# An mLSTM cell and a multiplicative FFN in one kernel: early steps reordered, weight words loaded ahead of the fifth unit's rows, one output pass of seven units on GpSimd

## The chip, the cores and the metric

The kernel runs on one NeuronCore of a Trainium2 chip. The metric is the device time of one execution in microseconds (us). Before the change three runs gave 424.96, 425.77 and 426.05 us, median 425.77 us.

## The reference

The inputs are q, k, v and o_gate of shape (4, 8, 768, 40), that is batch, heads, steps, head size; i_gate and f_gate of shape (4, 8, 768); and four weight matrices in float32. An mLSTM cell runs over the 768 steps and its result feeds a multiplicative feed-forward network:

```python
for t in range(S):
    m_new = np.maximum(f_gate[:, :, t] + m, i_gate[:, :, t])
    f_stab = np.exp(f_gate[:, :, t] + m - m_new)
    i_stab = np.exp(i_gate[:, :, t] - m_new)
    m = m_new
    C = f_stab[:, :, None, None] * C + i_stab[:, :, None, None] * np.einsum('bhd,bhe->bhde', vt, kt)
    n = f_stab[:, :, None] * n + i_stab[:, :, None] * kt
    h_tilde = np.einsum('bhde,bhe->bhd', C, qt)
    denom = np.maximum(np.abs(np.einsum('bhd,bhd->bh', n, qt)[:, :, None]), 1.0)
    y[:, :, t] = sigmoid(o_gate[:, :, t]) * h_tilde / denom
...
x = y.transpose(0, 2, 1, 3).reshape(3072, 320)
out = ((x @ w1) * (x @ w2) @ w3) @ w_out        # d_ff = 1024
```

## The kernel before

**Units and stages.** The 768 steps are cut into six chunks of 128. A unit is one chunk of one batch entry with all eight heads; unit n is chunk n // 4 of batch n % 4, and there are 24. The loop at line 820 runs over 32 stages s. In stage s TensorE makes the score products q·k of unit s and its contribution to the state, the output products of unit s - 1, the transposes of y of unit s - 2 (`x_trans`), the transposes of k and q of a coming unit (`turn`), and blocks of the FFN. The instructions of each engine run in the order in which they are written; on TensorE this is tied down by `in_order` (line 84).

**What one unit passes through.** SyncE issues the loads of k, q, v (`load`, line 136) and of the output gate (`load_o`, line 151). `turn` transposes k and q on TensorE and ScalarE copies the result out of PSUM. `rows_of_u` (VectorE, line 293) and `weights` (ScalarE, eight Exp instructions, line 298) make the decay weights `pw`, which `masks` (GpSimd, line 305) cuts to a triangle. `weighted` (GpSimd, line 327) makes v times its weight. In `quarter_work` (line 338) TensorE makes the scores `ss` and the state part `pc`; VectorE multiplies scores and weights (line 397); one stage later TensorE makes `ph` and `pi` from them. `outputs` (line 419) then works on VectorE: `h` from `pi` and `ph` (lines 423 to 430), the denominator in three small instructions (lines 438, 440, 441), and two full passes over 128 x 320 elements (lines 443 and 445): gate times reciprocal, then times h, which is y. `decayed` (GpSimd, line 333) and an add on VectorE (line 406 or 404, then 414) move the state on. `twice` (GpSimd, line 475) copies the last 64 columns of y, so that the third transpose of `x_trans` reads 128 columns; ScalarE copies the transposed result into xT (line 486).

**The steps of a denominator are a generator.** `outputs` returns a function `den`; each call of it issues the next step. `quarter_work` calls it between the instructions of the state.

**Weights.** The weight matrices are float64 (a float32 array times a float64 scalar), so each value comes as two 32-bit words, and the kernel makes float32 of them. Each 512 KB piece is loaded (`fetch`, SyncE), its two words are scaled (`scale`, lines 191 and 193 or 195: two ScalarE instructions, or one of ScalarE and one of VectorE when `early`), and joined in two VectorE instructions (`to_f32`, lines 199 and 200; a pair is one `convert`). Of w1 and w2 there are ten pieces, called 0 to 9 here: 0 and 1 are w1, 2 and 3 are w2, 4 is the remaining rows of both, all for the first 512 columns; 5 to 9 are the same for the last 512. `up` (line 618) starts an FFN block: eight matmuls for `pa` (w1), eight for `pb` (w2); `up_rest` (line 631) adds the remaining rows (tile `wr`) in 32 small matmuls, ScalarE copies `pa` to `a_sb` (line 638) and VectorE multiplies (line 639). The blocks of stages 2 and 3 need pieces 0 to 4, those of stages 4 and 5 pieces 5 to 9.

**Fillers.** `warm(n, m, small)` (line 97) issues matmuls whose result nobody reads: n of 128 x (m x 128), and `small` of 64 x 64. Each is carried out as two passes, two rows of the profile.

**Order before.** Piece 0 is scaled and converted in the prologue (lines 590, 592), piece 1 after `rows_of_u(1)` (lines 610, 611), both early. Stage 2 has a long insert, `between` (line 892): fillers, `x_trans(0)` and `x_trans(1)`, pieces 2 to 4, `turn(2)`, the first FFN block, and piece 5. SyncE's loads in stages 1 and 2 are listed at lines 825 to 838; the pieces 5, 6, 7 come ahead of k and q of unit 4, and 8 and 9 behind them. Pieces 6 and 7 are scaled and converted at the end of stage 2, 8 and 9 in stage 3 (`late`, lines 376 and 410).

Of the kernel before, what the change touches and what calls it, by code (L numbers as in the profile page):

```python
# [11 lines left out]
OP = mybir.AluOpType  # L12
# [4 lines left out]
def kernel(  # L17
# [92 lines left out]
    NB, NBQ, NBV = 4, 3, 5  # L110
    N_DVE = N_U = 10
    N_DIAG = 2
    q_all = const.tile([P, NBQ * H * DP], FP, name="q_all")
    qbuf = [q_all[:, i * H * DP:(i + 1) * H * DP].rearrange("p (h d) -> p h d", d=DP) for i in range(NBQ)]
    kbuf = [const.tile([P, H, DP], FP, name=f"kbuf{i}") for i in range(NB)]
# [222 lines left out]
    def quarter_work(s, rest, between, late):  # L338


        rest()

        def part(j, c0, n):
            return cell[j][:, :, c0:c0 + NP * n].rearrange("p x (n d) -> p x n d", d=n)

        ss, pc, pi = part(0, 0, L), part(0, NP * L, D1), part(1, 0, D1)
        ph = [cell[1][:, x, NP * D1:2 * NP * D1].rearrange("p (h d) -> p h d", d=D1) for x in range(2)]
        n = s - 1
        if 0 <= n < NU:
            pw, vt, qT = u_t.pop(n), vbuf[n % NBV], qT_t.pop(n)  # L350
            before = before_t.pop(n)
            if n < N_DIAG:
                warm(1)

            if n < N_DIAG:
                ph = mps([P, H, D1], "ph")
                for hq in range(H):
                    for r in halves:
                        mm(ph[r, hq, :], pw[r, hq, :], vt[r, hq, :])
            for hd in range(H // 2 if n >= N_DIAG else 0):  # L360
                for x, e in quarters:
                    hq = hd if x == e else hd + H // 2
                    mm(ph[x][halves[e], hd, :], pw[halves[x], hq, :], vt[halves[x], hq, :])
            for p in range(NP):
                for hip, x in quarters if n >= B else quarters[1:3]:
                    mm(pi[halves[x], hip, p, :], qT[heads[hip], p, halves[x]], before[x][heads[hip], p, :])
        den = None
        if 0 <= s - 1 < NU:
            den = outputs(s - 1, pi, ph)
            den()  # L370
            if between:
                for _ in range(3):
                    den()
                den = None
                between()
            if late:
                late()
        n, first_read = s, None
        if n < NU:
            c, b = divmod(n, B)  # L380
            kt, vw = kbuf[n % NB], vw_t.pop(n)
            ends = range(2 if c < NT2 - 1 else 1)
            first, second, after = state[b]
            before_t[n] = first, second
            state[b] = after, second, first
            kT, qT, pw = kT_t.pop(n), qT_t[n], u_t[n]
            for p in range(NP):
                for hip, x in quarters:
                    mm(ss[halves[x], hip, p, :], kT[heads[hip], p, halves[x]], qT[heads[hip], p, halves[x]])
            M = D if n else L  # L390
            for p in range(NP):
                for x, e in quarters:
                    if x in ends:
                        mm(pc[e * L:e * L + M, x, p, :], kt[halves[x], 2 * p + e, 0:M], vw[halves[x], 2 * p + e, :])
        if n < NU:
            pv = pw.rearrange("p (n two) t -> p two n t", two=2)
            first_read = nc.vector.tensor_tensor(out=pv, in0=ss, in1=pv, op=OP.mult)
        with tc.issue_after(first_read.ins) if first_read else nullcontext():
            if den:
                den()  # L400
            if n < NU:

                if c:
                    nc.vector.tensor_tensor(out=second, in0=pc[:, 0], in1=second, op=OP.add)  # L404
                else:
                    nc.vector.tensor_copy(out=second, in_=pc[:, 0])
                if len(ends) > 1:
                    decayed(after, second, n, 1)
            if late:
                late()  # L410
            if den:
                den()
            if n < NU and len(ends) > 1:
                nc.vector.tensor_tensor(out=after, in0=pc[:, 1], in1=after, op=OP.add)
            if den:
                done = den()
        return done if den else first_read

    def outputs(n, pi, ph):
        c, b = divmod(n, B)  # L420
        hs = slice(b * H, (b + 1) * H)
        h = sb.tile([P, H, D1], FP, name="h", tag="h")
        nc.vector.tensor_tensor(out=h.rearrange("p (n two) d -> p two n d", two=2), in0=pi,
                                in1=gT[:, c, hs].rearrange("p (n two) -> p two n", two=2).unsqueeze(3)
                                .to_broadcast([P, 2, NP, D1]), op=OP.mult)
        if n < N_DIAG:
            nc.vector.tensor_tensor(out=h, in0=ph, in1=h, op=OP.add)
        for x, e in quarters if n >= N_DIAG else ():
            part = h[halves[x], 0:H // 2] if x == e else h[halves[x], H // 2:H]
            nc.vector.tensor_tensor(out=part, in0=ph[x][halves[e]], in1=part, op=OP.add)  # L430

        den = sb.tile([P, H, 1], FP, name="den", tag="den")

        def steps():
            V = nc.vector
            yield V.tensor_scalar(out=den.bitcast(U32), in0=h[:, :, D:D1].bitcast(U32), scalar1=0x7FFFFFFF, scalar2=None,
                            op0=OP.bitwise_and)
            yield V.tensor_scalar(out=den, in0=den, scalar1=1.0, scalar2=2.0, op0=OP.max, op1=OP.mult)  # L440
            yield V.reciprocal(out=den, in_=den)
            e = o_t.pop(n)
            nc.vector.scalar_tensor_tensor(out=e, in0=e, scalar=1.0, in1=den.to_broadcast([P, H, D]), op0=OP.add, op1=OP.mult)
            y_t[n] = sb.tile([P, DM + REM], FP, name="y", tag="y")
            yield nc.vector.tensor_tensor(out=y_t[n][:, 0:DM].rearrange("p (h d) -> p h d", d=D), in0=h[:, :, 0:D],
                                           in1=e, op=OP.mult)

        done = steps()
        return lambda: next(done)

# [155 lines left out]
    cols_of_u()  # L606
    nc.scalar.copy(out=decay.rearrange("p j c -> p (j c)"), in_=pd)
    rows_of_u(1)
    nc.scalar.activation(out=g, in_=U, func=AF.Exp)
    scale_next(True)  # L610
    convert()

    ffn = ctx.enter_context(tc.tile_pool(name="ffn", bufs=2))


    ab_t = {}

    def up(gr, fs, cs):


        if gr not in ab_t:
# [3 lines left out]
        for p, wt in ((pa, w1), (pb, w2)):  # L625
            for i, f in enumerate(fs):
                for cc in range(KF):
                    mm(p[:, i, :], wt[:, cc, f * 128:(f + 1) * 128], x[:, cc, cs], start=(i == cc == 0), stop=False)
        return pa, pb, x, gr, fs, cs

    def up_rest(pa, pb, x, gr, fs, cs):
# [188 lines left out]
    for s in range(len(n_up)):  # L820
# [3 lines left out]
            load_u(s + 3)  # L824
        if s < 3:
            if s == 2:
                for _ in range(3):
                    fetch(*todo.pop(0))
            load(s + 2, slice(0, 2))
            if s == 1:  # L830
                load_o(2)
            if s == 2:
                for _ in range(2):
                    fetch(*todo.pop(0))
                fetched = 10
            load(s + 2, slice(2, 3))
            if s:
                load_o(s + 2)
        elif s + 2 < NU:
            load(s + 2)  # L840
            load_o(s + 2)
# [36 lines left out]
            seven[0]()  # L878
        now = [ups.pop(0) for _ in range(n_up[s])]
        open_ups = [up(*x) for x in now] if s != 2 else []  # L880
        if s == 3:
            turn(3)
        def rest():
            for x in open_ups:
                up_rest(*x)
# [6 lines left out]
        def between():  # L892
            twice(1)
            weighted(2)
            rows_of_u(3)
            for _ in range(3):
                scale_next()
            for n in range(2):
                x_trans(n)
                if n == 0:  # L900
                    warm(1, small=38)
            for _ in range(3):
                convert()
            turn(2)
            block = up(*now[0])
            weighted(3)
            weights(3)
            masks(3)
            out_gate(2)
            convert()  # L910
            up_rest(*block)

        gated = None
        if s <= NU:
# [3 lines left out]
        with tc.issue_after(gated.ins) if gated else nullcontext():  # L918
# [5 lines left out]
                ab_sums(*summed.pop(0))  # L924
            if NY <= s - 2 < NU:
                x_turn(s - 2)
            for n in () if s == 1 else (s + 2,) if s < B else (s + 2, s + 3) if s == B else (s + 3,):
                if n < N_U:
                    rows_of_u(n)
            if N_DVE <= s + 1 < NU:  # L930
# [3 lines left out]
            if s < len(n_up) - 2 and n_out[s + 1] and s > NU + 2:  # L934
                ab_sums(*summed.pop(0))
        if s == 0:
            weighted(1)
            weights(1)
            masks(1)
            gate_cols(g, gT, nc.scalar.copy)  # L940
# [5 lines left out]
        if s + 1 < N_DVE:  # L946
            while turned < min(s - 1, NY):
                x_trans(turned)
                turned += 1
            if s not in (1, 2):  # L950
                turn(s + 1)
        if s < NU:
            if 0 < s < NU - 1 and s != 2:
# [3 lines left out]
                if 2 < s < N_DVE:  # L957
                    twice(s - 1)
                masks(s + 1)
            if s != 2:  # L960
                out_gate(s)
        if s in (16, 17):
            weight_sums(s - 16)
        if s == B:
# [47 lines left out]
```

## Time and profile before

| what | value |
|---|---|
| runs, us | 424.96, 425.77, 426.05 |
| span of the profiled execution, us | 425.8 (the page gives no other time of it) |
| TensorE matmul busy | 414.1 us, 97% |
| VectorE busy | 313.5 us, 74% |
| ScalarE busy | 150.1 us, 35% |
| GpSimd busy | 154.3 us, 36% |
| HBM read and written | 44.50 and 5.80 MB |

Shares are of the span. PE is TensorE's matmul side, PEld its weight loads, DVE VectorE, ACT ScalarE, POOL GpSimd, SPq SyncE's queue of DMA issues. A matmul row of the profile is one pass. A releaser called "issue" means that the engine waited for nothing that the profile shows. Times in the text without a unit are us from the start of the span.

### The profile page before, as it was taken

What the parts mean: (1) busy time and instruction counts of PE and PEld (TensorE: products, weight loads), DVE (VectorE), ACT (ScalarE), POOL (GpSimd) and SP (SyncE); (2) the same over time, 40 slices, a digit from 0 to 9 for tenths busy, and PEclk for the clock granted to TensorE, in tenths of its full rate; (3) what the DMA queues carried; (4) which work ended last, traced back from release to release, by engine and by line L of the source; (5) the groups of instructions that cost most, each with busy time, mean ns of one, the idle gap of its engine ahead of it and who ended that gap; (6) DMA issues with size and microseconds to landing.
All of it is one profiled execution on the core that took longest, in us unless ns stands there. A gap on an engine that the chain in (4) does not pass through costs nothing.

```text
span 425.8 us, 13079 instructions
## 1 busy us (share of the span) xinstructions
PE 414.1 (97%) x5353; PEld 335.3 (79%) x5353; DVE 313.5 (74%) x635; ACT 150.1 (35%) x404; POOL 154.3 (36%) x211
## 2 busy tenths in 40 slices
PE   7989989999999999999999999999999999999996
PEld 4768878888688788787777778788778879888896
DVE  6676986888949779778736966596868699575971
ACT  4766865567723623630433313032311110210000
POOL 4421342233303303303307751546453587542100
PEclk9989999999999999999999999999999999999999
DMA  8999998598977776985425675756421120000001
GB/s 186 204 173 245 214 144 140 134 193 180 215 183 154 166 182 135 181 164 105 89 80 130 153 141 121 142 133 117 87 44 36 35 39 2 31 2 31 2 32 62
DMA packets 135211, 51.15 MB, mean 120 GB/s; under 512 B 109360, under 2 KB 126960, under 8 KB 135152
## 3 DMA queue, kind: packets, MB, share of 16 engines
q1 hardware_dynamic: 131552, 46.29, 53.9%
q10 hardware_dynamic: 3600, 4.03, 2.7%
q8 instruction: 42, 0.69, 0.7%
q14 instruction: 17, 0.14, 0.1%
HBM read 44.50 MB, written 5.80 MB: 118 GB/s over the span
## 4 chain that ended last, share of the span: by engine, by line
PE 53%; issue 20%; DVE 7%; POOL 7%; SPq 7%; DMA 5%; ACT 1%; POOLq 0%; DVEq 0%
PE cell L92 17%; PE pa L92 12%; PE o L92 8%; PE pb L92 8%; PE p L92 3%; POOL pw L308 3%; SPq L184 3%; DVE w3T L666 2%; PE pt L95 1%; POOL vw L330 1%; SPq L148 1%; DMA raw<-in_moe_w_dram 1%; PE fill L92 1%; POOL raw L659 1%; POOL state L335 1%
## 5 line engine op out<-in xcount | busy, mean ns | idle before, releaser
L335 POOL TENSOR_TENSOR state<-state,decay 128x164 f32<-128x164 f32 x40 | 20.0, 500 | 154.8 <-DVE state L404 129.0
L92 PE MATMUL pa<-xT,w 128*128 128x256 f32 x240 | 60.4, 382 | 0.0
L92 PEld LDWEIGHTS pa<-xT,w 128*128 128x128 f32 x240 | 44.4, 190 | 6.8 <-DVE h L430 0.4
L303 ACT ACTIVATE pw<-pw,aT 128x64 f32<-128x64 f32 x184 | 46.4, 339 | 3.2 <-ACT o_sb L741 1.9
L92 PE MATMUL pb<-xT,w 128*128 128x256 f32 x192 | 45.4, 379 | 0.0
L729 POOL TENSOR_TENSOR ab<-ab,a_sb 128x512 f32<-128x512 f32 x22 | 29.4, 1356 | 32.2 <-DVE ab L684 32.2
L92 PEld LDWEIGHTS pb<-xT,w 128*128 128x128 f32 x192 | 36.4, 190 | 5.0
L711 POOL TENSOR_TENSOR wo<-wo 128x512 f32<-128x512 f32 x22 | 27.4, 1268 | 29.8 <-DVE wo L686 29.8
L92 PE MATMUL pa<-xT,wr 64*64 64x256 f32 x384 | 37.0, 386 | 0.5 <-DVE wr L200 0.5
L92 PE MATMUL wp<-wo,w3T 128*128 128x320 f32 x128 | 35.9, 433 | 1.1 <-DVE ab L639 0.6
L308 POOL TENSOR_SCALAR_AFFINE_SELECT pw<-pw 64x512 f32<-64x512 f32 x48 | 35.8, 746 | 3.0 <-ACT pw L303 1.2
L92 PE MATMUL pb<-xT,wr 64*64 64x256 f32 x384 | 36.4, 380 | 0.0
L92 PE MATMUL cell<-w3o,ab 128*128 128x320 f32 x128 | 35.4, 432 | 0.0
L638 ACT ACTIVATE a_sb<-pa 128x512 f32<-128x512 f32 x24 | 14.3, 598 | 59.0 <-PE pb L92 59.0
L639 DVE TENSOR_TENSOR ab<-pb,a_sb 128x512 f32<-128x512 f32 x24 | 16.4, 688 | 23.2 <-ACT a_sb L638 22.8
L92 PEld LDWEIGHTS wp<-wo,w3T 128*128 128x128 f32 x128 | 23.8, 190 | 10.5 <-DVE ab L639 0.8
L92 PEld LDWEIGHTS cell<-w3o,ab 128*128 128x128 f32 x128 | 24.3, 190 | 9.5
L92 PEld LDWEIGHTS pa<-xT,wr 64*64 64x64 f32 x384 | 18.9, 132 | 15.4 <-issue 8.8
L686 DVE SCALAR_TENSOR_TENSOR a_sb<-pa,wo 128x512 f32<-128x512 f32 x12 | 8.3, 689 | 29.8 <-PE pa L92 29.8
L430 DVE TENSOR_TENSOR h<-cell,h 64x164 f32<-64x164 f32 x88 | 28.6, 326 | 1.6
L92 PE MATMUL po<-w3o,ab 128*128 128x320 f32 x96 | 26.4, 433 | 0.0
L92 PEld LDWEIGHTS po<-w3o,ab 128*128 128x128 f32 x96 | 18.1, 190 | 7.3
(180 smaller groups left out, 846.4 us busy)
## 6 DMA issues: line engine op xcount, KB each, us to landing
raw<-in_moe_w_dram SPq DMA_DIRECT2D x64, 128.0 KB, 3.4
kbuf<-in_k_dram SPq DMA_DIRECT2D x24, 160.0 KB, 4.5
v_all<-in_v_dram SPq DMA_DIRECT2D x24, 160.0 KB, 4.9
o_in<-in_o_gate_dram SPq DMA_DIRECT2D x24, 160.0 KB, 4.8
pw<-U_d SPq DMA_DIRECT2D x28, 128.0 KB, 3.5
raw<-in_moe_w_dram SPq DMA_DIRECT2D x5, 512.0 KB, 6.7
raw<-in_moe_w_out_dram SPq DMA_DIRECT2D x8, 320.0 KB, 4.1
gates<-in_k_dram SPq DMA_DIRECT2D x28, 80.0 KB, 2.5
```

Of the source, the lines that this page charges most:

```text
L92: in_order(nc.tensor.matmul(out, lhsT=lhsT, rhs=rhs, start=start, stop=stop))
L184: nc.sync.dma_start(out=dst, in_=src)
L303: nc.scalar.activation(out=pw[:, h, :], in_=src[:, h, :], func=AF.Exp, bias=aT[:, c, b * H + h:b * H + h + 1])
L308: nc.gpsimd.affine_select(out=pw[r], in_=pw[r], compare_op=OP.is_ge, fill=0.0, base=0, pattern=[[0, H], [1, L]], channel_multiplier=-1)
L335: nc.gpsimd.tensor_tensor(out=new, in0=old, op=OP.mult, in1=decay[:, b * NP:(b + 1) * NP, 2 * c + x:2 * c + x + 1] .to_broadcast([P, NP, D1]))
L430: nc.vector.tensor_tensor(out=part, in0=ph[x][halves[e]], in1=part, op=OP.add)
L638: nc.scalar.mul(out=a_sb, in_=pa, mul=UP ** -2)
L639: nc.vector.tensor_tensor(out=ab_t[gr][j][:, fs[0]:fs[-1] + 1, t0:t0 + a_sb.shape[-1]], in0=pb, in1=a_sb, op=OP.mult)
L666: nc.vector.tensor_tensor(out=dst, in0=p, in1=q, op=OP.subtract)
L686: nc.vector.scalar_tensor_tensor(out=out, in0=p, scalar=UP ** -2, in1=q, op0=OP.mult, op1=OP.add)
L711: aside_by.tensor_tensor(out=kept[j][:, 1:4:2], in0=kept[j][:, 1:3], in1=kept[j][:, 3:4].to_broadcast([128, 2, TH]), op=OP.add)
L729: aside_by.tensor_tensor(out=t[:, f:FO:FH, :], in0=t[:, f:FO:FH, :], in1=a, op=OP.mult)
```

## The change

The change has these parts.

1. In the prologue the scaling and conversion of piece 1 go; `rows_of_u(2)` and `weighted(1)` come instead (from stage 0). At the end of stage 0 ScalarE scales pieces 1 and 2, one ahead of `out_gate(0)` and one behind it, with both halves on ScalarE.
2. In stages 0 and 1 y of the unit is finished ahead of the state's second add (line 414). The filler ahead of the output products of unit 1 has 256 columns, not 512.
3. `between` is reordered: 8 small fillers ahead of `x_trans(0)`; then 2 of 512 columns and 10 small ones where there were 1 and 38; pieces 1 to 4 are converted in a row, then `rows_of_u(3)`; `turn(2)` stands between `pa` and `pb` of the first block; `up_rest` stands ahead of piece 5.
4. SyncE loads pieces 5 to 9 ahead of k and q of unit 4; the gate of unit 3 comes behind these instead of in stage 1. `turn(4)` moves from the end of stage 3 to the middle of stage 4, behind `up`.
5. For units 2 to 8 GpSimd multiplies h by the reciprocal, in place, ahead of `decayed`, and VectorE makes y in one pass. Line 441 comes ahead of line 404 there.

```diff
+    N_POOL = 9
...
             if n < N_DIAG:
-                warm(1)
+                warm(1, 4 >> n)
...
             if den:
                 den()
+                if on_pool(s - 1):
+                    den()
             if n < NU:
...
-            if den:
+            if den and not on_pool(s - 1):
                 den()
+            if den and n < 2:
+                done = den()
             if n < NU and len(ends) > 1:
                 nc.vector.tensor_tensor(out=after, in0=pc[:, 1], in1=after, op=OP.add)
-            if den:
+            if den and n >= 2:
                 done = den()
         return done if den else first_read
+
+    def on_pool(n):
+        return N_DIAG <= n < N_POOL
...
-            yield V.reciprocal(out=den, in_=den)
+            done = V.reciprocal(out=den, in_=den)
             e = o_t.pop(n)
-            nc.vector.scalar_tensor_tensor(out=e, in0=e, scalar=1.0, in1=den.to_broadcast([P, H, D]), op0=OP.add, op1=OP.mult)
             y_t[n] = sb.tile([P, DM + REM], FP, name="y", tag="y")
-            yield nc.vector.tensor_tensor(out=y_t[n][:, 0:DM].rearrange("p (h d) -> p h d", d=D), in0=h[:, :, 0:D],
-                                           in1=e, op=OP.mult)
+            y, hn, all_d = y_t[n][:, 0:DM].rearrange("p (h d) -> p h d", d=D), h[:, :, 0:D], den.to_broadcast([P, H, D])
+            if not on_pool(n):
+                yield done
+                V.scalar_tensor_tensor(out=e, in0=e, scalar=1.0, in1=all_d, op0=OP.add, op1=OP.mult)
+                yield V.tensor_tensor(out=y, in0=hn, in1=e, op=OP.mult)
+            else:
+                nc.gpsimd.tensor_tensor(out=hn, in0=hn, in1=all_d, op=OP.mult)
+                yield done
+                yield V.scalar_tensor_tensor(out=y, in0=e, scalar=1.0, in1=hn, op0=OP.add, op1=OP.mult)
...
     rows_of_u(1)
+    rows_of_u(2)
     nc.scalar.activation(out=g, in_=U, func=AF.Exp)
-    scale_next(True)
-    convert()
+    weighted(1)
...
-    def up(gr, fs, cs):
+    def up(gr, fs, cs, halfway=None):
...
+            if halfway and p is pa:
+                halfway()
...
             if s == 2:
-                for _ in range(3):
-                    fetch(*todo.pop(0))
-            load(s + 2, slice(0, 2))
-            if s == 1:
-                load_o(2)
-            if s == 2:
-                for _ in range(2):
+                for _ in range(5):
                     fetch(*todo.pop(0))
                 fetched = 10
+            load(s + 2, slice(0, 2))
+            if s:
+                load_o(s + 1)
             load(s + 2, slice(2, 3))
-            if s:
-                load_o(s + 2)
+            if s == 2:
+                load_o(4)
...
-        if s == 3:
-            turn(3)
+        if s in (3, 4):
+            turn(s)
...
             twice(1)
             weighted(2)
+            warm(0, small=8)
+            x_trans(0)
+            scale_next()
+            warm(2, small=10)
+            x_trans(1)
+            scale_next()
+            for _ in range(4):
+                convert()
             rows_of_u(3)
-            for _ in range(3):
-                scale_next()
-            for n in range(2):
-                x_trans(n)
-                if n == 0:
-                    warm(1, small=38)
-            for _ in range(3):
-                convert()
-            turn(2)
-            block = up(*now[0])
+            block = up(*now[0], halfway=lambda: turn(2))
             weighted(3)
             weights(3)
             masks(3)
             out_gate(2)
+            up_rest(*block)
             convert()
-            up_rest(*block)
...
-            for n in () if s == 1 else (s + 2,) if s < B else (s + 2, s + 3) if s == B else (s + 3,):
+            for n in () if s < 2 else (s + 2,) if s < B else (s + 2, s + 3) if s == B else (s + 3,):
...
         if s == 0:
-            weighted(1)
             weights(1)
             masks(1)
...
-            if s not in (1, 2):
+            if s not in (1, 2, 3):
                 turn(s + 1)
...
+            if s == 0:
+                scale_next()
             if s != 2:
                 out_gate(s)
+            if s == 0:
+                scale_next()
```

## The prediction

> **What bounds the kernel.** Page first: PE is busy 414.1 of 425.8 us. Then TensorE's waits over the whole run, because 97% busy leaves 11.7 us and the question is where they are.
>
> ```profile
> PE 414.1 (97%) x5353; PEld 335.3 (79%) x5353; DVE 313.5 (74%) x635; ACT 150.1 (35%) x404; POOL 154.3 (36%) x211
> ...
> q8 instruction: 42, 0.69, 0.7%
> ```
> ```profile
> PE cell L92 <- issue: 1.9, 2, 1.5
> PE fill L92 <- POOL ident masks.py:199: 1.6, 1, 1.6
> PE px L95 <- DVE y L445: 1.2, 1, 1.2
> PE wp L92 <- DVE ab L639: 0.6, 1, 0.6
> PE wp L92 <- issue: 0.5, 1, 0.5
> PE pa L92 <- DVE wr L200: 0.5, 1, 0.5
> ```
>
> The same question from 60 us on finds 2.0 us (0.6 + 0.5 + 0.4 + 0.3 + 0.2). So the change can gain only ahead of 60: by a shorter wait, or by less filler, which counts as busy. TensorE's timeline there:
>
> ```profile
> 22.96 0.83 PE L95 MATMUL px<-ident,y 128*128 128x128 f32 x3 [1.19 <-DVE y L445]
> 23.59 4.90 PE L92 MATMUL fill<-ident 128*128 128x512 f32 x78
> 28.41 0.55 PE L95 MATMUL px<-ident,y 128*128 128x128 f32 x3
> ...
> 47.33 0.43 PE L92 MATMUL pa<-xT,wr 64*64 64x256 f32 x1 [0.51 <-DVE wr L200]
> ...
> 59.05 0.35 PE L92 MATMUL cell<-vw,kbuf 64*40 64x41 f32 x12 [1.49 <-issue]
> ```
>
> Look at the second row: 78 filler passes hold TensorE for 4.9 us. The windows of 1 us show why so long: the granted clock fell after the wait.
>
> ```profile
> 22.00:23.00 1.00, 0.04 (x1) 0.04 (x1) 0.97 (x3) 0.98 (x3) 0.57 (x1) 1.00 1.46 157
> ...
> 24.00:25.00 1.00, 1.00 (x2) 0.00 (x0) 0.83 (x4) 1.00 (x3) 0.00 (x0) 0.50 1.13 167
> 25.00:26.00 1.00, 1.00 (x11) 0.57 (x12) 0.97 (x3) 1.00 (x3) 0.24 (x1) 0.50 0.90 150
> ```
>
> Behind the engine columns stands the clock: 0.50 from 23.4 to 26.8. I follow the change to one checkpoint, stage 4's `wr` matmuls (47.33), behind which TensorE is nearly full.
>
> **Prologue.** VectorE loses L193 0.49, L199 0.81 and L200 0.69 and gains a 0.70 transpose ahead of L397 of unit 0, which then waits for `masks(0)` (12.91 + 1.45 = 14.36) instead of starting at 15.29: 0.9 earlier. `ph` of unit 0 can follow from 15.75, the end of its filler, instead of 16.07. But TensorE next stops for "issue" until 18.22, a stop that VectorE does not set, so `ss` of unit 1 ends at 19.26 as before: gain 0. `weighted(1)` needs v of unit 1, landed at 13.8 (8.92 + 4.9), so it does not block GpSimd.
>
> **y of units 0 and 1.** L414's wait (0.54) and its 0.25 leave y(0)'s chain, and GpSimd's masks no longer double L443 and L445 (0.86, 0.82 beside them; 0.49 each in unit 1): y(0) 22.91 to about 21.6. `h` of unit 1 then waits for `pi` (21.78): y(1) 25.62 to 24.8. The halved filler saves nothing, `ph(1)` waits for L397 (19.99).
>
> **What takes that back.** ScalarE now scales piece 2 (landed 10.73 + 7.4 = 18.1) ahead of `weights(2)`: two rows, 1.1 by their pitch (22.40, 22.95, 23.52). So `weights(2)` starts at 20.1 instead of 18.99 and `masks(2)` ends near 23.6 instead of 22.58. `twice(0)` stands behind it on GpSimd, and `px(0)`'s third transpose reads its copy: 23.9 instead of 23.34. The eight fillers (0.5) fit in before that.
>
> **Fillers.** Now 4 wide and 20 small passes. At full clock a wide one takes 0.44 (0.88 for two), at half 0.88; a small one 0.03 at full clock (76 in 2.9 us, 1.4 of it at half). Full: 1.76 + 0.6, so `px(1)` at 26.3. Half until 26.8: 27.7. Before: 28.41. Since `turn(2)` (0.87) no longer lies between `px(1)` and `pa`, the xT copy (0.48) is bare: `pa` at 27.3 or 28.7 against 29.67, and with `turn(2)` inside, `wr` at 31.6 or 33.0 against 33.22. VectorE keeps up: four converts of 1.16 from 24.8, and 0.45 for one beside `weighted(2)` (1.13 for 0.69 at 26.69), end at 29.9.
>
> **What is late next.** Piece 5 is now scaled behind `a_sb`, which is behind `weights(3)`, which needs `rows_of_u(3)`, now after four converts. ScalarE: 30.6 + 2.0 + 0.4 + 0.6 = 33.5 (full clock) or 35.0 against 33.08. With before's own spacing, L397 of unit 2 comes at 35.4 or 36.9 (35.60), piece 7 is done at 40.2 or 41.7 (40.42), and then L639, `h` and piece 8 take 3.84 (41.32 to 45.16): 44.0 or 45.6. `pb` of stage 4 needs piece 8 from its second matmul. Before, `turn(4)` stood ahead of it and filled the time; now TensorE is there at 42.2 and waits. Then 1.5 of `pb`, 0.87 of `turn(4)`, `wr`: 46.4 (46.8 where GpSimd's new pass slows piece 9's convert), or 48.1, against 47.33. **-0.7 or +0.8.**
>
> **The loads.** No DMA is added. Pieces 8 and 9 land ahead of unit 4's rows, about 38 and 40.5 (estimate: piece 7 at 29.72 + 6.9 = 36.6, less 1.1 for the gate taken out, plus 2 to 3 each as before), no longer the last cause. k and q of unit 4 move from 37.8 and 39.4 to about 42.8; `turn(4)` at 45 or later covers that by 2. The gate of unit 3, near 44, is read by `out_gate(3)` (48.48 before); late, it would hold the `kT` copies behind it on ScalarE. Piece 9's buffer is piece 1's, free at 26 now; its load is issued after 30.
>
> **GpSimd's pass.** VectorE saves one of two passes (0.76 + 0.49 becomes 0.5 to 0.76). GpSimd gains a product of 320 columns, 0.74 by `weighted` (328 columns). It is queued ahead of `decayed`, for which L414 waits; y is behind L414. At 73.4: before y ends at 75.85; after, L441 ends 73.7, product 74.5, `decayed` 74.95, L414 75.25, y 75.75 to 76. Nothing gained, and y has cover (done 48.74, read at 50.05). Value 0; bounds -0.6 (the one wait for L639, 0.58) and +0.7 (a full GpSimd product on the path once).
>
> **Instruction blocks.** The "issue" stops have a pattern: 42 instruction packets of 16 KB stand against 10,706 matmul and weight rows, 255 for each. Counting the trace's TensorE rows (semaphore rows too), the four stops lie at rows 448, 1984, 3264 and 4544, each 192 above a multiple of 256. So TensorE stops where a block of 256 runs out ahead of the next one's arrival, in runs of tiny matmuls: with stops taken out, the blocks before the last three ran in 2.45, 2.75 and 2.45 us and cost 1.49, 0.30 and 0.54; two others of 3.47 and 1.92 cost nothing. The change has 38 passes and 38 weight loads fewer in `between`, so every later boundary falls 76 rows later. Counted so, eight blocks run in under 3.5 us (1.88, 1.89 and 2.09 the shortest, at about 79, 123 and 170). At the mean of those five, 0.47, that is 3.7 instead of 2.3: **+1.4**. Bounds: all stops gone, -2.3; or each block waits until 3.3 us after its start (mean of the three that stopped), 7.1 in all, +4.8. I take the mean, since the rows of equal length differ by three times.
>
> The Trainium skill ("Runtime: NRT & Kernel Launch", "Instruction fetch mechanics") has blocks of 256 instructions and calls the crossing mostly hidden; that would make this term 0, but 1.49 at row 1984 shows that it is not hidden here.
>
> The skill ("TensorE: Matmul & The Clock Gate", "What's actually happening") has half clock after an idle window of 3413 ns, windows free-running against the kernel. The trace's 3.4 us agrees; by the free phase both of my clock cases could occur in the same program, and it speaks against thinning the fillers.
>
> **Sum.** Profiled span 425.8, the median of the runs 425.77: no correction. Full clock: -0.7, +1.4, 0: **426.5**.
>
> **Rivals.** *Boundaries fall well*: the stop at 57 goes (-1.5), none comes, and -0.7: 423.6, or 423.0 with the wait for L639 gone. For it: row 1984 falls on sparse matmuls after the shift. Against: eight short blocks. *Half clock*: the wait for `twice(0)` (1.3) ends in a half-speed window, +0.8 for -0.7: 428.0; it decides once the window that holds 20 to 23.4 is again too idle. For it: the same window did so before, and has less filler now. *Block stops, the slower side*: at full clock and 7.1 us of stops, 429.9; slower by over 1.3 from 0.54 us a block on. *The change does not do what it says*: y early, but `px(0)` still waits on GpSimd; this is in my sum, and if `twice(0)` is not late, `px(1)` comes 0.5 earlier, which piece 8 hides.
>
> **Chances.** Forecast 0.38 (its own range 425 to 428), boundaries well 0.30, half clock 0.20, block stops 0.12. 0.3% is 1.3 us, about what a measurement of this kernel can tell from no change. Faster: 0.28 + 0.03 = 0.31; same 0.02 + 0.27 = 0.29; slower 0.08 + 0.20 + 0.12 = 0.40. Range 422.6 to 430.0: from 0.4 under the fast rival's 423.0 to the block rival's end.
>
> **What would show it.** Right: `px(0)`'s third pass waits for L476 near 23.9; `pb` of stage 4 waits for L200 for over 1 us; `wr` of stage 4 at 46 to 48 without a wait; "issue" stops at rows 192 above multiples of 256, none at 57, one near 79 or 123; L414's wait grows from 0.47 to about 0.9 for units 2 to 8. Wrong: no wait at `pb`, or stops elsewhere.

## The result and the profile after

| | before | after |
|---|---|---|
| median, us | 425.46 | 430.33 |
| runs, us | 424.66 to 428.25 (7) | 428.38 to 432.26 (7) |
| span of the profiled execution, us | 425.8 | 429.9 |
| mean granted clock there | 0.996 | 0.991 |

The ratio is 1.0115, 95% interval 1.0080 to 1.0151: the change costs about 4.9 us. The prediction said 426.5 with a range to 430.0; it was wrong. A run's time is 1.9 to 2.4 us above its span (432.18 beside 429.9 here), so the execution of before that was profiled took about 428, as its longest run of seven did, and not 425.77.

The page of after, busy times and instruction packets:

```profile
PE 415.2 (97%) x5315; PEld 336.1 (78%) x5315; DVE 309.4 (72%) x627; ACT 150.2 (35%) x405; POOL 160.7 (37%) x218
...
q8 instruction: 42, 0.69, 0.7%
```

TensorE issues 38 passes fewer and is busy 1.1 us longer, VectorE has lost 4.1 us of work, and neither says why the span grew by 4.1. TensorE's waits do (total, times, longest):

```profile
PE cell L92 <- issue: 5.0, 4, 1.8
PE fill L92 <- POOL ident masks.py:199: 1.6, 1, 1.6
PE px L95 <- issue: 1.3, 1, 1.3
PE wp L92 <- DVE ab L655: 0.6, 1, 0.6
PE pa L92 <- ACT xT L500: 0.6, 1, 0.6
```

The stops put down to "issue" were 2.7 us before (1.9 and 0.5 in its waits, 0.3 at 96.5) and are 6.3 now: 3.6 of the 4.1 us. The single wait on y, 1.2 before, is gone. TensorE's timeline after has the stops and the checkpoint:

```profile
18.61 0.62 PE L92 MATMUL cell<-qT,kT 40*64 40x64 f32 x26 [1.45 <-issue]
24.29 0.90 PE L95 MATMUL px<-ident,y 128*128 128x128 f32 x3
24.98 3.30 PE L92 MATMUL fill<-ident 128*128 128x512 f32 x24
28.21 0.55 PE L95 MATMUL px<-ident,y 128*128 128x128 f32 x3
29.33 1.99 PE L92 MATMUL pa<-xT,w 128*128 128x256 f32 x8 [0.57 <-ACT xT L500]
...
48.92 0.43 PE L92 MATMUL pa<-xT,wr 64*64 64x256 f32 x1 [0.44 <-DVE wr L201]
...
84.97 0.23 PE L92 MATMUL cell<-vw,kbuf 64*40 64x41 f32 x2 [1.78 <-issue]
...
130.66 0.23 PE L92 MATMUL cell<-vw,kbuf 64*40 64x41 f32 x1 [1.28 <-issue]
...
178.42 0.27 PE L95 MATMUL px<-ident,y 128*128 128x128 f32 x1 [1.29 <-issue]
```

The fifth stop is 0.50 at 43.17. By the count of TensorE's rows in the trace the five stand at rows 448, 1216, 2752, 4032 and 5312, each again 192 above a multiple of 256; the stop at row 1984 (59.05 before) is gone. The second thing that differs is the clock. Windows of 1 us (PE, PEld, DVE, ACT, POOL, clock, DMA share, GB/s) show it at half from 19.5, behind the first stop, to 26.4, two windows of 3.4 us where before had one:

```profile
19.00:20.00 1.00, 1.00 (x50) 0.95 (x40) 0.30 (x1) 1.00 (x3) 0.00 (x0) 0.77 1.12 212
20.00:21.00 1.00, 1.00 (x8) 0.35 (x9) 0.89 (x5) 1.00 (x5) 0.15 (x1) 0.50 0.98 93
...
26.00:27.00 1.00, 1.00 (x4) 0.36 (x2) 0.97 (x3) 0.85 (x2) 0.61 (x2) 0.81 1.36 145
```

Behind the longer first stop, the second window and the stop at 43, the checkpoint of the prediction, `wr` of stage 4, is at 48.92 against 47.33.

### The profile page after: what moved, and what is told of

It is laid out like the page before. It is cut to its first block, busy times and chain, and to the rows that moved or that the text cites. A ratio compares the mean times of both kernels' runs of the same rounds, so it can differ in the third digit from the quotient of the medians.

```text
span 429.9 us, 13003 instructions
## 1 busy us (share of the span) xinstructions
PE 415.2 (97%) x5315; PEld 336.1 (78%) x5315; DVE 309.4 (72%) x627; ACT 150.2 (35%) x405; POOL 160.7 (37%) x218
## 4 chain that ended last, share of the span: by engine, by line
PE 88%; DVE 6%; issue 2%; ACT 1%; DMA 1%; SPq 0%; POOL 0%; DVEq 0%; ACTq 0%
PE cell L92 22%; PE pa L92 21%; PE pb L92 14%; PE wp L92 8%; PE o L92 8%; PE po L92 5%; PE p L92 4%; PE px L95 2%; DVE w3T L682 1%; PE pt L95 1%; PE fill L92 1%; DVE pw L786 1%; PE ph L92 1%; ACT pw L304 0%; DMA out_dram<-o_sb 0%
## 5 line engine op out<-in xcount | busy, mean ns | idle before, releaser
L92 PE MATMUL pb<-xT,w 128*128 128x256 f32 x192 | 45.6, 380 | 0.0
L438 DVE TENSOR_TENSOR h<-cell,h 64x164 f32<-64x164 f32 x88 | 28.7, 326 | 1.6
L92 PE MATMUL po<-w3o,ab 128*128 128x320 f32 x96 | 26.4, 434 | 0.0
```

Of the source, the lines that this page charges most:

```text
L92: in_order(nc.tensor.matmul(out, lhsT=lhsT, rhs=rhs, start=start, stop=stop))
```

## The experiments

Four theories. **A**: blocks of 256 TensorE rows; the change moved every boundary behind 28 us by 76 rows, and three now fall in runs of tiny matmuls. **B**: the reordered early part and its half-clock windows. **C**: GpSimd's pass. **D**: the order of the loads, with TensorE held by piece 8. Fillers are used as the probe: their results are read by nobody, and a small one is four rows (two passes, two weight loads). "No window" below are the runs whose mean clock shows no half-clock window (0.999 or 1.000; one window of 3.4 us takes it to 0.996, as in before's profile). Before has a median of 425.49 in 68 such runs of 117 (three of 476 us and more are left out), after 428.72 in 6 of 14.

**Rows back, rows gone.** The first puts the 76 rows back into after, the second takes 76 from before and changes nothing else.

```diff
             x_trans(1)
+            warm(0, small=19)
```
```diff
-                    warm(1, small=38)
+                    warm(1, small=19)
```

> The changed kernel with 19 more small fillers behind the second x transpose: 76 TensorE rows, so that every later instruction boundary lies where it lay before the change. They cost 1.1 us of filler, of which 0.57 lies in the wait for the xT copy. Theory A (instruction blocks): the stops of 1.78, 1.28 and 1.29 us at about 84, 130 and 178 us go, the stop at row 1984 comes back with up to 1.5, so some 2 to 3 us under the changed kernel, 426.5 to 428.5. Theory B (the early reordering itself lost the time, through the half clock and through piece 8): 430 to 431, since the early part is as it was and has more filler. Theory C (GpSimd's pass): no change either, 430 to 431.

Measured: 429.63, ratio 1.0074 [1.0036, 1.0112]; no window, two runs: 426.9. The median contradicted A, the runs at full clock did not; left open here and taken up below.

> The kernel before with 19 small fillers instead of 38 and nothing else: 76 rows fewer, so the boundaries lie as in the changed kernel, with all the old order. Theory A: stops of over 1 us near 80, 125 and 172 us, and 2 to 3 us slower than before, 427.5 to 428.5. Theory B and C: at most 1 us faster, from the shorter filler, or no difference, 424.5 to 425.5.

Measured: 428.71, ratio 1.0074 [1.0034, 1.0114]; no window 427.42. Taking out 19 fillers brings `wr` of stage 4 to 45.92, 1.4 earlier, and costs 3 us. Its timeline and windows show both halves of it, a stop at row 2752 (the row of after's stop at 84.97), and half clock behind it:

```profile
82.38 0.19 PE L92 MATMUL cell<-vw,kbuf 64*40 64x41 f32 x1 [2.13 <-issue]
```
```profile
82.00:83.00 1.00, 0.62 (x6) 0.50 (x6) 0.32 (x1) 0.00 (x0) 0.00 (x0) 1.00 0.55 201
...
84.00:85.00 1.00, 1.00 (x4) 0.74 (x3) 0.75 (x2) 1.00 (x5) 0.91 (x2) 0.50 0.79 168
85.00:86.00 1.00, 1.00 (x4) 0.82 (x3) 0.75 (x2) 1.00 (x6) 0.08 (x1) 0.50 1.23 230
```

**GpSimd's pass** taken out of after, and put alone into before (the hunks of part 5):

```diff
-    N_POOL = 9
+    N_POOL = 2
```

> The changed kernel without GpSimd's pass (no unit takes it); all else stays, TensorE's rows too. Theory A: the time of the changed kernel within 0.5 us, 430, with the same stops. Theory C: back by 1 us or more, 429 or less. Theory B: no difference.

Measured: 432.18, ratio 1.0141 [1.0099, 1.0184], stops of 0.73, 1.22, 1.55 and 1.30. Without the pass after is no faster, so C is not the cause of the loss.

> The kernel before with GpSimd's pass for units 2 to 8 alone. TensorE's rows stay. Theories A and B: the same as before within 0.6 us, since y had cover and the add of the state waits longer by about what the pass saves. Theory C (the pass costs time): 427 or more.

Measured: 427.30, ratio 1.0027 [0.9997, 1.0058]. Its waits and VectorE's timeline show a price at one place:

```profile
PE pa L92 <- DVE wr L201: 1.3, 1, 1.3
```
```profile
45.14 0.97 DVE L200 TENSOR_SCALAR wr<-raw 128x512 uint32<-128x512 uint32 x1
```

The convert of piece 9 runs beside GpSimd's product (45.11, 0.72) and takes 0.97 where the one of piece 8 takes 0.43, so `wr` waits 1.3, not 0.5.

**Loads alone**: the hunks of part 4, put into before.

> The kernel before with part 4 alone: pieces 5 to 9 ahead of k and q of unit 4, the gate of unit 3 behind them, the transposes of unit 4 in the middle of stage 4. TensorE's rows keep their number, so boundaries behind stage 4 stay. Theory A (instruction blocks explain the loss): within 1 us of before, 424.6 to 426.6. Theory D (this part costs time, because piece 8's convert now holds TensorE in stage 4): 426.7 or more. The part's own purpose would show as 0.5 us less, the wait for the second half of wr gone.

Measured: 426.16, ratio 0.9992 [0.9967, 1.0017]: no difference. D falls as a cause by itself.

**Other alignments.** In this order: after with 24 rows fewer in `between`, before with 16 fewer, after with 64 more ahead of `x_trans(0)`:

```diff
-            warm(2, small=10)
+            warm(2, small=4)
```
```diff
-                    warm(1, small=38)
+                    warm(1, small=34)
```
```diff
-            warm(0, small=8)
+            warm(0, small=24)
```

> The changed kernel with 4 small fillers instead of 10 ahead of the second x transpose: 24 rows fewer still, so the boundaries lie 24 rows later. By a count with 3.6 us from a block's first row to the next block's arrival, the stops behind 50 us sum to 0.9 instead of 3.9: theory A expects 427.5 or less. Theory B: the same or slower, 430 to 431, as less filler means no more clock. Theory C: 430.

Measured: 427.21, ratio 1.0027 [0.9994, 1.0061]. Six fillers less, and most of the loss is gone; the only stops are 0.38 and 0.18.

> The kernel before with 34 small fillers instead of 38: 16 rows fewer. By the count of blocks that run in under 3.6 us, the stops near 92, 139 and 185 us go and the one at 57 stays: theory A expects 0.5 to 1 us less than before, 424.5 to 425. Theory B: no difference, 425.5.

Measured: 426.48, ratio 0.9993 [0.9966, 1.0021]. The stops at 96 and 144 went, as counted, and the one at 59 stayed (1.64); yet the time is the same, since waits for `w`, `qT` and `wr` stand in their place.

> The changed kernel with 24 small fillers instead of 8 ahead of the first x transpose: 64 rows more, 0.5 us at full clock, in a wait of 1.2 us for GpSimd's copy. Boundaries move to where few blocks run short (one near 56 us is left). Theory A: 3 us under the changed kernel, 427 to 427.5, as with 4 small fillers further on. Theory B (half-clock windows around 20 us cost it): besides, more runs at full clock, as TensorE is idle for less; with both, 426. If neither holds: 430.

Measured: 428.99, ratio 1.0055 [1.0015, 1.0094]; no window 426.54. The median is above A's 427 to 427.5. The late stops went; new ones came early, 1.81 us inside the fillers at row 704 and 1.07 at 61.

**Aligned versions of before.** Both hold the loads of part 4 and move rows in two places; the second has 22 for 44 and stage 6 for stage 7:

```diff
-                    warm(1, small=38)
+                    warm(1, small=44)
...
+            if s == 7:
+                warm(0, small=12)
```

> The kernel before with the change's loads (its part 4, measured at 426.2, no difference), 24 TensorE rows more between stage 2's transposes (6 small fillers of 4 rows) and 48 rows more (12 small fillers) at the end of stage 7: work that computes nothing, put in only to move where blocks of 256 rows begin. Theory A (instruction blocks): by the count of rows the boundaries then fall among long matmuls, at most one stop of about 0.5 us is left where before has 1.5, 0.3 and 0.5, so the span falls by 1 to 1.7 us, less about 0.7 for the added matmuls if they lie on the path: 424.8 to 425.8. Theory B (early reordering and half clock) and theory D (loads): nothing here that could gain, and the added rows cost: 426.2 to 427.

> The kernel before with the change's loads (its part 4), 64 TensorE rows fewer between stage 2's transposes (16 small fillers less) and 48 rows more (12 small fillers) at the end of stage 6, so 16 fewer from there on. Theory A (instruction blocks): the rows as counted leave the late boundaries where the run with 16 rows fewer had none of its late stops, and move the one at about 58 us away: 424.5 to 425.5. Theory B: 64 fewer fillers alone, as in the kernel before with 76 fewer, cost 1.5 to 2 us, whatever comes later: 427.5 to 428.5. Theory D: 426.2 as with the loads alone.

Measured: 425.67, ratio 1.0004 [0.9973, 1.0035], and 425.33, ratio 0.9986 [0.9960, 1.0013]. As counted, one stop is left in each, 0.50 and 0.52. Both times are inside A's range, but before was at 426.12 beside them, so with 2.2 of its 2.7 us of stops gone no gain is shown. Their runs without a window are a little lower (425.03 in eight and 424.19 in three, against 425.49 in 17 of before's 35 beside them). Counting rows tells the stops, not the whole time.

**Aligned versions of the change.** The first is after with few fillers and ScalarE's scaling back behind the gate, the second has parts 1 to 3 alone, without parts 4 and 5:

```diff
-                warm(1, 4 >> n)
+                warm(1)
...
-            warm(2, small=10)
+            warm(2, small=4)
...
-            if s == 0:
+            if s == 1:
                 scale_next()
```
```diff
-    N_POOL = 9
+    N_POOL = 2
...
-            warm(2, small=10)
+            warm(2, small=4)
```

> The kernel after with 6 small fillers less (24 rows, as in the run with few fillers, 427.2), the filler of unit 1 wide again, and ScalarE's scaling of pieces 1 and 2 back behind the gate of its stage, as close to before as part 3 lets it. Theory B (early reordering and half clock): ScalarE is free for twice(0) at about 23, px(0) comes at its time of before, the half-clock windows are as seldom as before: 425.0 to 426.0. Theory A alone (instruction blocks): the boundaries lie as in the run with few fillers, 426.8 to 427.6, and half-clock windows as often as there.

> The kernel after with 6 small fillers less (24 rows), without the loads' part and without GpSimd's pass: parts 1 to 3 alone, at the boundaries of the run with few fillers (427.2). Theory C (GpSimd's pass) and theory D (loads, piece 8 holds TensorE): what is left above before is theirs, so 425.3 to 426. Theory A (instruction blocks) and B (early part): neither part costs anything, 427 to 427.8; without the pass on GpSimd the time is rather higher by up to 1, since the four passes come back on VectorE.

Measured: 426.41, ratio 1.0027 [0.9994, 1.0060], and 426.01, ratio 0.9970 [0.9939, 1.0002]. The first lies between the ranges of B and A, and its ratio is that of the run with few fillers, so undoing the ScalarE edits is worth nothing that shows. The second is nearer what C and D expected (425.3 to 426) than A's 427 to 427.8: without parts 4 and 5 it is 0.4 us under the first, which was measured beside it (0.3 in the runs without a window), and 1.2 under the run with few fillers, measured at another time. The intervals of the ratios overlap, so a price of these two parts together is neither shown nor excluded. The interval of the second just takes in no change, so no version is shown to beat before. In the first, TensorE's timeline shows what the prediction expected of piece 8:

```profile
43.30 1.56 PE L92 MATMUL pb<-xT,w 128*128 128x256 f32 x6 [1.67 <-DVE w L201]
...
46.18 0.43 PE L92 MATMUL pa<-xT,wr 64*64 64x256 f32 x1 [0.44 <-DVE wr L201]
```

**Late rows only.** The open question was whether the late stops are worth their size with the early part untouched:

```diff
+            if s == 6:
+                warm(0, small=15)
```

That is 60 rows more in after, 1.1 us of TensorE by the trace.

> The kernel after, its early part untouched, with 60 TensorE rows more (15 small fillers) behind the wr matmuls of about 69.5 us: all that comes later then lies 16 rows ahead of before, where no late boundary falls in a run of tiny matmuls. Theory A (instruction blocks): the stops of 1.78, 1.28 and 1.29 us at 85, 131 and 178 go, the added rows cost about 1.0, so 430.3 - 4.35 + 1.0 = 427.0, and 425.5 where no half-clock window falls. Theory B (the early reordering and its half-clock windows) and D (loads): the late part is not to blame, 430.5 to 431.3.

Measured: 427.76, ratio 1.0040 [1.0018, 1.0062]; no window 426.0 in four runs. A's numbers were 427.0 and 425.5, B's and D's 430.5 and more. TensorE's waits and its timeline:

```profile
PE cell L92 <- issue: 1.6, 2, 1.0
```
```profile
18.49 0.62 PE L92 MATMUL cell<-qT,kT 40*64 40x64 f32 x26 [1.02 <-issue]
...
28.11 0.55 PE L95 MATMUL px<-ident,y 128*128 128x128 f32 x3
29.23 1.99 PE L92 MATMUL pa<-xT,w 128*128 128x256 f32 x8 [0.57 <-ACT xT L500]
43.13 0.52 PE L92 MATMUL cell<-vw,kbuf 64*40 64x41 f32 x32 [0.57 <-issue]
48.82 0.43 PE L92 MATMUL pa<-xT,wr 64*64 64x256 f32 x1 [0.43 <-DVE wr L201]
```

Up to 48.8 it is after to within 0.15 us, half clock included (two windows). Behind that no stop is left: the three blocks that ran in 1.89, 1.89 and 1.99 us in after run in 3.13, 3.12 and 3.12 here, and cost nothing. Its span is 425.8, 4.1 under after's, although it does 1.1 us more work. Adding work made the kernel faster.

**The undo again, and after again**, both unchanged.

> The kernel after with its 76 rows back behind the second transpose of stage 2, once more, for its profile. Theory A: boundaries from 28 us on as in before, so stops of about 1.5, 0.3 and 0.5 at 58, 96 and 144, and none at 85, 131 and 178; at 17 to 18.6, ahead of the added rows, anything from 0.4 to 1.45; the rest over before is the added matmuls' 1 us or a half-clock window: 427 to 429.6. Theory B or D: the profile shows 2 us or more of waits on VectorE or ScalarE ahead of 60 us that before does not have, with the wr matmuls of stage 4 later than 48.

Measured: 427.87, ratio 1.0034 [1.0003, 1.0065]; no window 427.2 in eight of twelve runs. So the first undo run's 429.6 was mostly half-clock windows (seven of its nine runs had them). Its stops lie at before's rows; the one at row 1984 did not occur this time, although that block ran in 2.45 us, as in before:

```profile
17.59 0.62 PE L92 MATMUL cell<-qT,kT 40*64 40x64 f32 x26 [0.38 <-issue]
...
47.02 0.43 PE L92 MATMUL pa<-xT,wr 64*64 64x256 f32 x1 [0.44 <-DVE wr L201]
...
94.44 0.38 PE L95 MATMUL pt<-ident,q_all 128*128 128x128 f32 x2 [0.38 <-issue]
...
142.88 4.20 PE L92 MATMUL wp<-wo,w3T 128*128 128x320 f32 x15 [0.99 <-issue]
```

> The kernel after once more, unchanged, for a second profile and more runs beside the other two. Theory A: stops at the same rows, about 85, 131 and 178 us, of 1.2 to 1.8 us each; the median 429.5 to 430.5, 428.8 without a half-clock window. Theory B: the late stops are chance of one execution and move or vanish, while the wr matmuls of stage 4 stay at 48.9 against 47.3.

Measured: 430.33, ratio 1.0095 [1.0060, 1.0130]. The profiled execution had a span of 435.0 and a mean clock of 0.980, so only the place of its stops is used: the same three rows.

```profile
86.09 0.23 PE L92 MATMUL cell<-vw,kbuf 64*40 64x41 f32 x2 [1.72 <-issue]
...
134.10 0.23 PE L92 MATMUL cell<-vw,kbuf 64*40 64x41 f32 x1 [1.59 <-issue]
...
183.56 0.27 PE L95 MATMUL px<-ident,y 128*128 128x128 f32 x1 [1.30 <-issue]
```

## Why the prediction was wrong, by its own steps

**The block stops: right mechanism, wrong size.** The step that failed is "At the mean of those five, 0.47, that is 3.7 instead of 2.3: +1.4". The stops came at rows 192 above multiples of 256, none at 57, and at the three shortest blocks, given as about 79, 123 and 170 us (their runs ended at 83, 129 and 177). They cost 1.78, 1.28 and 1.29, 4.35 in all. The count of eight was right as well: behind 60 us eight blocks of after ran in under 3.5 us (1.90, 3.13, 1.89, 1.99, 2.23, 2.35, 3.00 and 2.88). But the loss was not spread over them as a mean has it: three stopped and five cost nothing. That the mean gave 3.7 for what came to 4.35 is near by luck; the late stops alone are +2.0 instead of +1.4. The rest was missing from the term, which counted only short blocks: the stop at 18 (behind a block of 5.03 us) cost 1.04 more than before, and a new one at 43 (behind one of 6.98 us) 0.50. In all the term is +3.6. The upper bound had the price of a stop about right (TensorE on again 3.3 us after the block's start; 3.87, 3.36 and 3.54 in after, 2.8 to 4.4 in the other profiles where the block ran in under 3 us), but it charged it eight times.

What tells the blocks with a stop from those without is in the traces: the 42 instruction packets on q8. Taken in order, the first goes with the block that runs out at row 448, the second with the one that runs out at 704, and so on. In the 16 profiles (without that of the first undo run, whose span was 476.7) 41 waits of TensorE are put down to "issue". All stand where a block runs out, and each ended 1.26 to 1.79 us after the end of that block's packet; in after, at row 2752, the packet ended at 83.69 and TensorE went on at 84.97. Behind 50 us 37 blocks ran in 2.6 us or less. In 21 the packet began 0.3 to 1.7 us behind the block's first row, and TensorE stopped for 0.4 to 2.1 us at the end of each (one of these waits is put down to ScalarE). In 16 it began 0.1 to 3.7 us ahead of that row, and there was no stop. So in after the three came 1.31, 0.59 and 0.73 behind and the other five of the eight 0.19 to 3.69 ahead; in the late-rows run the three blocks at those rows had theirs 2.91 to 3.74 ahead; in before the block of 1.92 us that cost nothing had its packet 2.91 ahead, and at row 1984 it came 1.68 behind in before and 1.35 ahead in the undo run that had no stop there. What puts a packet ahead of its block or behind it was not tested.

That these stops carry most of the loss is shown by the late-rows run. The Trainium skill ("Runtime: NRT & Kernel Launch", "Instruction fetch mechanics") calls the crossing mostly hidden; in after it was hidden at all but five of 42 boundaries, and the five cost 6.3 us.

**The stop at 18 and the clock.** "But TensorE next stops for 'issue' until 18.22 [...] gain 0" did not foresee that the stop itself varies, though the number of rows ahead of it is the same in all these kernels: none in eight of the sixteen profiles, 0.4 to 1.0 in seven, 1.45 in after's. Where it was 0.9 or more (after, late rows, after again) half clock began between 18.5 and 19.6 and lasted two windows or more; where it was 0.84 or less there was one window, from 22 or 23 on, or none. So the half-clock rival had a path the prediction lacked, a block stop, beside the wait for `twice(0)` that it named. This is a coincidence seen in three executions, one of them that of 435.0 us, and not an experiment on it.

**The early part.** Predicted and measured in after: y(0) 21.6 and 22.2; `masks(2)` 23.6 and 23.58; `px(1)` 27.7 (half clock) and 28.21; `pa` 28.7 and 29.33; `wr` of stage 2 33.0 and 33.86; L397 of unit 2 (L398 now) 36.9 and 37.42; piece 8 done 45.6 and 46.0; `wr` of stage 4 48.1 and 48.92. The chain is right. All of it except `masks(2)` is late by 0.4 to 0.9, which the longer half clock and the stop at 43 can account for. The wait of `px(0)` for GpSimd's copy is there in the undo run (1.12, until 22.99); in after TensorE came to it only at 24, at half clock, and did not wait. At full clock the checkpoint was predicted at 46.4 to 46.8; the undo run has 47.02, the run with ScalarE's edits back 46.18 and the one with few fillers 45.63. The wait of `pb` for piece 8, "over 1 us", is 1.67 in the run with ScalarE's edits back; in after the stop at 43 stands in its place. "-0.7" is not earned by the reordering alone: the kernel before with 76 rows fewer reaches 45.92, and its two aligned versions 45.59 and 46.20, without it.

**The loads.** k and q of unit 4 landed at 42.2 and 43.0 (42.8 given), the gate of unit 3 at 43.7 (44). Put alone into before, the loads cost nothing that shows, 0.9992.

**GpSimd's pass.** The wait of L414 (L419 now) grew from 0.47 to 1.06 (0.9 given), and y has cover. The value in after is not above the resolution (with 1.0115, without 1.0141). Put alone into before it gave 1.0027, no difference that is shown; its profile has the convert doubled ahead of `wr`, which the prediction had at 0.4 in passing.

**"Profiled span 425.8, the median of the runs 425.77: no correction."** Wrong: the profiled execution took about 428, some 2.5 above the median, with a half-clock window that most runs of before do not have. The terms were added to a span and the sum was given as a time, which are 1.9 to 2.4 apart.

**What stays open.** Of the 4.9 us, 3.2 show at full clock (428.72 against 425.49), and the late rows bring these down to 0.5 with 1.1 of added work. The other 1.7 goes with windows at half clock, which are more frequent in after: 8 of 14 runs against 49 of 117. That block stops set some of them off fits three traces of stops at 18, two of stops near 84 and one at 134, but was not tested by itself. Nor is it settled why before's aligned versions lose their stops and keep their time. Before's own stops may vary: at row 1984 its profile has 1.49, the one with GpSimd's pass 0.54, and the second undo run none. Whether parts 4 and 5 together cost a little is open too.

## What to carry to other kernels

In a kernel bound by an engine with thousands of tiny instructions, count that engine's rows ahead of every edit, and look where blocks of 256 end before and after it: an edit that takes out work can cost more than it saves, far behind the place of the edit. Price a stop by the time the block that ran out took and by its instruction packet, not by a mean over blocks: short blocks whose packet began ahead of their first row cost nothing here. And tell what an edit does apart from where it moves the blocks: give its rows back with fillers, at the place of the edit and then late, and compare versions whose late stops are gone.

## What the runs showed of the hardware

- Eleven blocks of 256 TensorE rows that ran in 1.9 to 2.0 us had their instruction packet (in order, as above) begin 0.4 to 1.5 us behind their first row, and all ended in a stop of 1.2 to 2.1 us (rows 2752, 4032 and 5312 of after, after again and no pool; 2752 and 4032 of rows gone, the last put down to ScalarE). Four as short had the packet 2.9 to 3.7 us ahead and no stop (row 6592 of before, loads, pool and the second undo run). Blocks of 3.1 us and more cost nothing behind 60 us. Between lie both: 2.59 without a stop (few fillers, row 3520), 2.66 with one of 0.2 to 0.5.
- Taking 38 passes and 38 weight loads out of before cost 0.7%.
- A stop of 2.13 us, well short of a window of 3.4, was followed 1.5 us later by half clock for 3.4 us (rows gone); one of 1.78 at 84.97 in after was not.
- VectorE's 128x512 word pass took 0.97 us instead of 0.43 beside a GpSimd product of 0.72 us.
